# Row maxima by direct transfer, and the first head's steps first, in a pooled attention and MLP kernel

## Chip, core and metric

The kernel runs on one core of a Trainium2 chip. The metric is the time of one execution on the device in microseconds (us), as the median of several runs. The engines named below are TensorE (PE in the profile, its weight loads PEld), VectorE (DVE), ScalarE (ACT), GpSimd (POOL) and SyncE (SP), which issues every transfer.

## The reference

```python
# q, k, v: (4, 8, 1152, 64) float32; w_in: (512, 2048), w_out: (2048, 512), float64 as drawn
q_pool = q.reshape(B, H, S // 2, 2, D).mean(axis=3)          # 576 queries per head
scores = q_pool @ k.transpose(0, 1, 3, 2) / sqrt(D)          # 576 x 1152
scores = scores - max(scores, axis=-1)
attn = exp(scores); attn = attn / (sum(attn, axis=-1) + 1e-9)
x = (attn @ v) -> (4 * 576, 8 * 64) = (2304, 512)
h = x @ w_in
out = maximum(0.01 * h, h) @ w_out                           # (2304, 512)
```

## The kernel before

There are 32 heads (4 batches of 8). Matmuls run on float32r operands, and float32 accuracy is kept by splitting an operand into a high and a low part. For each head:

- `load_k`, `load_q` and `load_v` (L397, L435, L489) bring keys, queries and values. `k_tr` (L401) transposes the keys on TensorE in nine blocks of 128 keys. `k_hi` (L417) writes the rounded high part of the keys to the tile `ka`, `k_lo` (L421) the low part into the other 64 partitions: even blocks of keys have the high part in partitions 0 to 63, odd blocks in 64 to 127. `k_dup` (L425) copies the high parts to a tile `kb` by three transfers.
- `q_sum` (L454) adds pairs of queries on GpSimd, `q_tr` (L459) transposes them, `q_hi` (L470) rounds the high part into both halves of `qh`, `q_lo` (L474) writes the low part to `ql`.
- The row maxima. `qk` (L495) computes scores with queries on the partitions: four tiles of 128 consecutive queries against three thirds of the keys, and the last 64 queries, twice side by side, against two quarters from each half of the keys. `vmax` (L511) takes the maximum of each score tile on VectorE, `m_side` (L514) moves the last tile's second half of maxima on ScalarE, and `vneg` (L518) takes the negated maximum of all partial ones into `neg`, with the query on the partition and the tile number along the row. `m_tr` (L521) transposes `neg` on TensorE, `m_cp` (L525) copies five rows of 128 from the bank to `ms` on ScalarE, and `m_dma` (L529) writes them, by one transfer, to row 64 of `ql`. Row 64 of `kb` is 1, so the maximum is subtracted inside the score matmul.
- The scores again, now with keys on the partitions: `qkt` (L537, matmuls L542 and L543), `exp` (L545) on ScalarE, `esum` (L549) on GpSimd for the row sums, `pv` (L554) with the values, `r_mm` (L565) for the sums of what `esum` left, and a chain of small transfers (`r_fold`, `r_row`, `r_wide`) by which the output is divided by the sums.

The weights come as float64, are converted on ScalarE and VectorE (`w_f32`, L624) and split (`w_hi`, `w_lo`), beside the first heads. Four of nine MLP blocks (`l1`, `post`, `l2`) run beside the later heads, the others after them.

The order of the work is written out before anything runs, by a planner (`Scheduler`, L130). Each step has a priority, in units in which a head has 5, a duration that the planner assumes, steps it depends on, and buffers it takes. The planner repeatedly picks the startable step of the lowest priority and gives it to an engine that may do it. `SHIFT` (L45) adds an offset to the priority of each kind of step, by phase. Every engine then executes its instructions in that fixed order and waits on semaphores. The tag `t` stands for the two or three banks that `k_tr`, `q_tr`, `qk`, `m_tr` and `r_mm` share, `s` for the score banks of `qkt`.

Of the kernel before, what the change touches and what calls it, by code (L numbers as in the profile page):

```python
# [9 lines left out]
F32 = mybir.dt.float32  # L10
# [10 lines left out]
AHEAD = 14  # L21
MAXES = 4
# [4 lines left out]
MT = 5  # L27
# [18 lines left out]
    "esum": (-3.5, 20.75, 83.5, -27.75, -12.25),  # L46
    "exp": (27.75, 25.75, -8.25, -9, 17.25),
    "g_act": (0, 0, 6, 10),
    "g_hi": (0, 0, -18, -14),
    "g_lo": (0, 0, 13.25, -16),  # L50
    "g_mix": (0, 0, 24),
    "k_dup": (4.25, -32.25, -78.5, -3.75, 43.5),
    "k_hi": (24.5, 72.75, -4, -104, -22.5),
    "k_lo": (-45.5, -9, 0, 25.25, -34.25),
    "k_tr": (23.5, 16, 19.5, -24, 35),
    "l1": (-4.75, -27.5, -7.5),
    "l2": (-19, 22.25, 14),
# [24 lines left out]
    "r_cp": (-27.75, -22, -55, -0.5, -3),
    "r_fold": (1.75, 11, -65, -44, 19.5),
    "r_inv": (-6.25, 18.25, -2.75, 3.5, 16.5),
    "r_mm": (23, 28.5, -8.25, 2, 10.5),
    "r_row": (41.25, 19.75, -23.25, 6, 0.25),
    "r_wide": (-31.25, 0, 49.25, 7, -7.25),
    "scale": (21.25, -36.75, 8.5, 17.5, -7.5),
    "vmax": (-22.75, -29, -31, -139.5, 109.75),
    "vneg": (43.25, -29.75, 2, -29.5, -19.25),  # L90
    "w_f320": (-10, 37, -0.25, -37.5),
    "w_f321": (-37.5, 119.5, 44.75, -11.75),
    "w_f322": (-2, -36.5, 6.5, 53.5),
# [3 lines left out]
    "w_out_dma": (0.5, -1.5),
    "w_rest": (48.5, 7.5, -1.25),
    "w_sum": (-31, -3.75, 3.25),
    "w_top": (-3, -35.25, -3),  # L100
    "ws_load": (-30, -15, 45.75),
    "x_hi": (2, -12, 43.25),
    "x_lo": (-35.25, -26, 5.25),
    "x_load": (3.25, -11.75, 0.25),
    "x_out": (15.5, -21, -23.25, -41, 8),
    "zeros": (0, 58.25, -46),
}
PHASES = {"attention": (1, 2, 8, 14), "weights": (8, 16, 24), "mlp": (1, 3)}
# [21 lines left out]
class Scheduler:  # L130
# [76 lines left out]
    def start(self, s, e, at, pending):  # L207
# [44 lines left out]
def tile_pooled_attention_moe(  # L252
# [40 lines left out]
    def copy(e, out, in_):  # L293
# [4 lines left out]
    NBU = len(BURSTS)  # L298
    QTILES = [(c, min(128, SP - c)) for c in range(0, SP, 128)]
# [11 lines left out]
        "ms": (1, [NQ, 128], F32R, sb),  # L311
# [45 lines left out]
    negs = [sb.tile([128, D], F32, name=f"neg{i}") for i in range(2)]  # L357
# [51 lines left out]
    def by_half(t, x):  # L409
        return t[:, :(KT - 1) * 128].rearrange("p (a x n) -> p a x n", x=2, n=128)[:, :, x]  # L410

    def k_part(hd, x):
        if x == 2:
            return kps[hd, 1][0:64, :128], ka[hd][:, (KT - 1) * 128:], 0
        return kps[hd, 0][64 * x:64 * x + 64].rearrange("p (a n) -> p a n", n=128), by_half(ka[hd], x), 64 * x

    def k_hi(hd, x, e):  # L417
        src, d, o = k_part(hd, x)
        copy(e, d[o:o + 64], src)

# [133 lines left out]
    def pv(hd, b, e, *got):  # L554
# [304 lines left out]
    def sp(n, nbytes, run=512):  # L859
        return dict(eng={"SP": 0.45 * n}, lat=nbytes / 300e3 * max(1.0, 512 / run))  # L860

    for hd in range(NHD):
        p0 = 5.0 * hd
        pr = p0 - AHEAD
# [8 lines left out]
        for g in range(2):  # L873
# [4 lines left out]
            for x in (2,) if g else (0, 1):  # L878
                n = 128 if g else 512
                step(k_hi, hd, x, prio=pr + 0.1 * g, eng={"ACT": act(n, True)}, deps=[("k_tr", hd, g)])  # L880
                step(k_lo, hd, x, prio=pr + 0.1 * g, eng={"DVE": dve(n, psum=True)}, deps=[("k_hi", hd, x), None if g else ("k_hi", hd, 1)])
        step(k_dup, hd, prio=pr + 1, **sp(3, 0.3e6), deps=[("k_hi", hd, x) for x in range(3)], takes=[("kb", [last])])
        step(load_v, hd, prio=pr + 2, **sp(1, 0.3e6), order=after("load_v"), takes=[("vv", [("pv", hd, NBU - 1)])])
        step(load_q, hd, prio=pr - 4 - early, **sp(1, 0.3e6), order=after("load_q"), takes=[("qn", [("q_sum", hd)])])
# [6 lines left out]
        for x in range(2):  # L891
            for y in range(2):
                step(q_hi, hd, x, y, prio=pr + 0.5, eng={"ACT": act(HW, True)}, deps=[("q_tr", hd)])
# [3 lines left out]
        pm = p0 - MAXES  # L897
        ready = [("k_lo", hd, x) for x in range(3)] + [("q_hi", hd, x, y) for x in range(2) for y in range(2)]
        todo = [(i, c) for i in range(NQ) for c in range(NCH if QTILES[i][1] == 128 else 2)]
        for n, (i, c) in enumerate(todo):  # L900
            before = [("qk", hd, *todo[n - 1])] if n else after("qk", *todo[-1])
            w = CW if QTILES[i][1] == 128 else S // 4
            step(qk, hd, i, c, prio=pm + 0.02 * n, eng=mm(w) if w == CW else mm(w, w), deps=ready + before + ([] if w == CW else [("q_side", hd)]),
                 takes=[("t", [("vmax", hd, i, c)])] + ([] if n else [("st", [("m_tr", hd)])]))
            step(vmax, hd, i, c, prio=pm - 1 + 0.02 * n, eng={"DVE": dve(w, psum=True)}, deps=[("qk", hd, i, c)])
        step(m_side, hd, prio=pm - 2, eng={"ACT": act(2)}, deps=[("vmax", hd, *x) for x in todo[-2:]])
        step(vneg, hd, prio=pm - 2, eng={"DVE": 0.17}, deps=[("m_side", hd)] + [("vmax", hd, *x) for x in todo[:-2]])
# [3 lines left out]
        ready += [("k_dup", hd), ("m_dma", hd)] + [("q_lo", hd, x) for x in range(2)]  # L911
        done = ("pv", hd, NBU - 1)
        ns = KT - 1 - direct(hd)
        for t in range(KT):
# [3 lines left out]
            step(exp, hd, t, prio=p0 - 5 + 0.5 * t, eng={"ACT": act(2 * HW, True)}, deps=[("qkt", hd, t)],  # L918
# [152 lines left out]
```

## Time and profile before

| | |
|---|---|
| runs | 909.6, 913.74 and 913.08 us, median 913.08 us |
| profiled execution | 910.57 us |
| its span, from the first to the last instruction | 908.8 us |
| mean granted TensorE clock | 0.993 |
| TensorE busy | 873.0 us (96%), 6408 matmuls and as many weight loads |
| VectorE, ScalarE, GpSimd busy | 528.6 (58%), 464.0 (51%), 454.0 us (50%) |
| DMA packets | 113268, 158.73 MB; 21632 of them under 512 B |

Matmuls are pipelined, so a matmul's own length is longer than the distance between the starts of two in a row. An engine's idle time is put down to what ended it (the releaser).

### The profile page before, as it was taken

What the parts mean: (1) busy time and instruction counts of PE and PEld (TensorE: products, weight loads), DVE (VectorE), ACT (ScalarE), POOL (GpSimd) and SP (SyncE); (2) the same over time, 40 slices, a digit from 0 to 9 for tenths busy, and PEclk for the clock granted to TensorE, in tenths of its full rate; (3) what the DMA queues carried; (4) which work ended last, traced back from release to release, by engine and by line L of the source; (5) the groups of instructions that cost most, each with busy time, mean ns of one, the idle gap of its engine ahead of it and who ended that gap; (6) DMA issues with size and microseconds to landing.
All of it is one profiled execution on the core that took longest, in us unless ns stands there. A gap on an engine that the chain in (4) does not pass through costs nothing.

```text
span 908.8 us, 17344 instructions
## 1 busy us (share of the span) xinstructions
PE 873.0 (96%) x6408; PEld 731.1 (80%) x6408; DVE 528.6 (58%) x1135; ACT 464.0 (51%) x911; POOL 454.0 (50%) x351
## 2 busy tenths in 40 slices
PE   5899989899999999999999999999999999999997
PEld 3676666577778777887887787788888999999997
DVE  6788868687665455554544555404249963645443
ACT  3677777766666655555556555444124442323231
POOL 1467676686778685676667567567511010110000
PEclk9899999999999999999999999999999999999999
DMA  6478876757846764454355354444665676767670
GB/s 169 127 222 267 242 216 172 190 158 218 246 142 176 212 174 108 137 161 118 108 160 164 99 139 132 113 124 121 212 216 178 190 230 217 231 222 215 202 229 28
DMA packets 113268, 158.73 MB, mean 175 GB/s; under 512 B 21632, under 2 KB 80160, under 8 KB 113184
## 3 DMA queue, kind: packets, MB, share of 16 engines
q1 hardware_dynamic: 113184, 157.64, 58.8%
q8 instruction: 50, 0.82, 0.4%
q14 instruction: 34, 0.28, 0.1%
HBM read 130.02 MB, written 17.90 MB: 163 GB/s over the span
## 4 chain that ended last, share of the span: by engine, by line
PE 77%; DMA 9%; ACT 3%; POOL 3%; SPq 3%; issue 3%; DVE 2%; ACTq 0%; POOLq 0%; DVEq 0%
PE banks L703 21%; PE banks L560 11%; PE banks L784 11%; PE banks L509 8%; PE banks L542 7%; PE banks L543 6%; PE banks L816 3%; PE banks L818 3%; PE banks L817 3%; DMA raw<-in_moe_w_in_dram 3%; DMA ws<-wd 2%; POOL sm L552 2%; SPq L585 2%; PE banks L571 2%; PE banks L407 1%
## 5 line engine op out<-in xcount | busy, mean ns | idle before, releaser
L547 ACT ACTIVATE e<-banks 128x576 f32<-128x576 f32 x288 | 185.3, 650 | 174.3 <-PE banks L543 169.8
L552 POOL TENSOR_TENSOR sm<-sm,e 128x576 f32<-128x576 f32 x168 | 242.8, 1445 | 40.2 <-ACT e L547 31.1
L512 DVE TENSOR_REDUCE stat<-banks 128x1 f32<-128x384 f32 (+1 forms) x448 | 217.5, 534 | 71.2 <-PE banks L509 67.5
L542 PE MATMUL banks<-qh,ka 128*128 128x288 f32 x576 | 170.9, 312 | 3.0 <-ACT e L547 2.8
L543 PE MATMUL banks<-ql,kb 128*128 128x288 f32 x576 | 162.0, 297 | 1.1 <-DMA ql<-ms 1.1
L703 PE MATMUL banks<-xb,ws 128*128 128x256 f32 x1152 | 160.9, 283 | 0.8 <-DMA ws<-wd 0.7
L560 PE MATMUL banks<-e,vv 128*64 128x288 f32 x1152 | 154.1, 412 | 0.0
L703 PEld LDWEIGHTS banks<-xb,ws 128*128 128x128 f32 x1152 | 151.1, 189 | 2.6 <-DMA ws<-wd 0.9
L542 PEld LDWEIGHTS banks<-qh,ka 128*128 128x128 f32 x576 | 109.2, 190 | 28.4 <-issue 12.4
L560 PEld LDWEIGHTS banks<-e,vv 128*64 128x64 f32 x1152 | 76.8, 137 | 61.5 <-issue 15.1
L509 PE MATMUL banks<-ka,qh 128*128 128x384 f32 x384 | 115.1, 366 | 8.6 <-DVE stat L512 4.3
L423 DVE TENSOR_TENSOR ka<-banks,ka 64x512 fp32r<-64x512 f32 (+1 forms) x96 | 53.1, 554 | 104.4 <-ACT ka L294 89.0
L543 PEld LDWEIGHTS banks<-ql,kb 128*128 128x128 f32 x576 | 109.5, 190 | 2.6 <-DMA ql<-ms 1.3
L552 POOL TENSOR_TENSOR sm<-e 128x576 f32<-128x576 f32 x32 | 46.2, 1444 | 86.1 <-ACT e L547 86.0
L509 PEld LDWEIGHTS banks<-ka,qh 128*128 128x128 f32 x384 | 68.1, 194 | 23.8 <-DVE stat L512 10.4
L703 PE MATMUL banks<-ka,ws 128*128 128x256 f32 x576 | 71.9, 280 | 1.4 <-DMA ws<-wd 1.4
L703 PEld LDWEIGHTS banks<-ka,ws 128*128 128x128 f32 x576 | 69.8, 188 | 2.0 <-DMA ws<-wd 1.8
L784 PE MATMUL banks<-wo,gg 128*128 128x256 f32 x312 | 59.9, 282 | 0.0
L472 ACT ACTIVATE qh<-banks 64x288 fp32r<-64x288 f32 x128 | 51.7, 404 | 3.5 <-PE banks L465 2.1
L294 ACT CAST ka<-banks 64x512 fp32r<-64x512 f32 (+1 forms) x96 | 45.0, 470 | 13.7 <-PE banks L407 12.6
L457 POOL TENSOR_TENSOR qs<-qn 96x384 f32<-96x384 f32 x32 | 32.0, 1000 | 34.2 <-PE banks L465 22.0
L784 PEld LDWEIGHTS banks<-wo,gg 128*128 128x128 f32 x312 | 46.9, 188 | 0.1
(177 smaller groups left out, 1220.2 us busy)
## 6 DMA issues: line engine op xcount, KB each, us to landing
ws<-wd SPq DMA_DIRECT2D x144, 512.0 KB
kn<-in_k_dram SPq DMA_DIRECT2D x32, 288.0 KB
qn<-in_q_dram SPq DMA_DIRECT2D x32, 288.0 KB
vv<-in_v_dram SPq DMA_DIRECT2D x32, 288.0 KB
kb<-ka SPq DMA_DIRECT2D x64, 128.0 KB
raw<-in_moe_w_in_dram SPq DMA_DIRECT2D x16, 512.0 KB
wd<-ws SPq DMA_DIRECT2D x16, 512.0 KB
raw<-in_moe_w_out_dram SPq DMA_DIRECT2D x16, 512.0 KB
```

The lines of the kernel that those rows point to most:

```text
L294: ENG[e].copy(out=out, in_=in_) if e == "ACT" else ENG[e].tensor_copy(out=out, in_=in_)
L423: nc.vector.tensor_tensor(out=d[64 - o:128 - o], in0=src, in1=f32(d[o:o + 64]), op=ALU.subtract)
L472: nc.scalar.activation(out=q_half(qh[hd], x)[64 * y:64 * y + 64], in_=src, func=AF.Copy, scale=QSCALE)
L509: nc.tensor.matmul(p, lhsT=lhsT, rhs=ka[hd][:, k0:k0 + w], start=(j == 0), stop=(j == 128 // n - 1))
L512: nc.vector.tensor_reduce(out=mx[hd][:, i, c:c + 1], in_=mps.pop((hd, i, c)), axis=AX.X, op=ALU.max)
L542: nc.tensor.matmul(p[:, hf, :HW], lhsT=ka[hd][:, ks], rhs=qh[hd][:, c], start=True, stop=False)
L543: nc.tensor.matmul(p[:, hf, :HW], lhsT=kb[hd][:, ks], rhs=ql[hd][:, c], start=False, stop=True)
L547: nc.scalar.activation(out=ex[hd, t], in_=sps.pop((hd, t))[:, :, :HW], func=AF.Exp)
L552: ENG[e].tensor_tensor(out=sm[hd], in0=ex[hd, 0] if t == 1 else sm[hd], in1=ex[hd, t], op=ALU.add)
L560: nc.tensor.matmul(p[64 * hf:64 * hf + 64, :HW], lhsT=vv[hd][:, t, :], rhs=ex[hd, t][:, hf], start=(t == 0), stop=(t == KT - 1),)
L703: nc.tensor.matmul(p, lhsT=wst[i, f][:, a, c, :], rhs=xx[i][x][:, c, :], start=(n == 0), stop=(n == 3 * KC - 1))
L784: nc.tensor.matmul(o, lhsT=g[i, p][:, a], rhs=w[:, x], start=(p == 0 and n == 0 and half == 0), stop=(p == FH - 1 and n == 2), skip_group_ ...
```

## The change

The transpose and the copy of the maxima (`m_tr`, `m_cp`, the tile `ms`) go. `neg` is 8 columns wide instead of 64, and `m_dma` writes from it straight to the row by two transfers. To let 4 adjacent values of one partition lie side by side in the row, tile i of `qk` consists of the queries i, i + 4, i + 8 and so on, so its stationary operand has a step of four columns. Keys are laid out as two contiguous halves (even blocks, then odd blocks, the ninth block shared between them), so `k_dup` takes two transfers, the remainder is done in two pieces by `k_hi` and `k_lo`, and `pv` takes the value blocks in that order (`TILES`). `qk` goes through the first third of the keys for all tiles, then the side tile, then the last and the middle third, each with only the parts of the keys that it needs; `m_side` no longer waits for other maxima. For head 0, the priorities of preparation and maxima are lowered by 200, `load_q` comes first of all, and `k_hi` and `q_hi` may run on VectorE as well. Exponentials are kept in order. The planner assumes 0.5 us for an issue (0.45 before), another price for changing the array's tiling, and all of `SHIFT` has new values.

```diff
+START = 200
-MT = 5
+MBYTES = 0.2e6
...
+TILINGS = {"pv": 1, "r_mm": 2, "qkr": 3}
...
-            tiled = s.key[0] in ("pv", "r_mm")
-            if tiled and not self.tiled:
-                end = self.free[e] = end + SWITCH
-            self.tiled = tiled
+            tiling = TILINGS.get(s.key[0], 0)
+            if tiling != self.tiled:
+                end = self.free[e] = end + SWITCH / 2
+            self.tiled = tiling
...
+    TILES = [*range(0, KT, 2), *range(1, KT, 2)]
...
-    negs = [sb.tile([128, D], F32, name=f"neg{i}") for i in range(2)]
+    negs = [sb.tile([128, 8], F32, name=f"neg{i}") for i in range(2)]
...
+        if x < 2:
+            return kps[hd, 0][64 * x:64 * x + 64], ka[hd][:, 640 * x:640 * x + 512], 64 * x
+        y = x - 2
+        return kps[hd, 1][0:64, 64 * y:64 * y + 64], ka[hd][:, 512 + 64 * y:576 + 64 * y], 64 * y
...
-        nc.sync.dma_start(out=d[0:64, (KT - 1) * 128:], in_=s[0:64, (KT - 1) * 128:])
         for x in range(2):
-            nc.sync.dma_start(out=by_half(d, x)[0:64], in_=by_half(s, x)[64 * x:64 * x + 64])
+            c = slice(x * S // 2, (x + 1) * S // 2)
+            nc.sync.dma_start(out=d[0:64, c], in_=s[64 * x:64 * x + 64, c])
...
-                lhsT = qh[hd][:, o:o + n]
+                lhsT = qh[hd][:, i:n * (NQ - 1):NQ - 1]
...
-        nc.sync.dma_start(out=f32(ql[hd])[64:65].rearrange("p (i n) -> p i n", n=128), in_=f32(mst.pop(hd)))
+        row, full = f32(ql[hd])[64:65], 128 * (NQ - 1)
+        nc.sync.dma_start(out=row[:, :full].rearrange("o (n i) -> o n i", i=NQ - 1), in_=mng[hd][:, :NQ - 1])
+        nc.sync.dma_start(out=row[:, full:SP].rearrange("o (n i) -> o n i", i=1), in_=mng[hd][:SP - full, NQ - 1:NQ])
...
-        pr = p0 - AHEAD
+        pr = p0 - AHEAD - (0 if hd else START)
...
-        todo = [(i, c) for i in range(NQ) for c in range(NCH if QTILES[i][1] == 128 else 2)]
+        todo = [(i, 0) for i in range(NQ)] + [(NQ - 1, 1)] + [(i, c) for c in (2, 1) for i in range(NQ - 1)]
...
-        step(m_tr, hd, prio=pm - MT, eng=trs(128), deps=[("vneg", hd)], takes=[("t", [("m_cp", hd)])])
-        step(m_cp, hd, prio=pm - 2, eng={"ACT": act(128, True)}, deps=[("m_tr", hd)], takes=[("ms", [("m_dma", hd)])])
-        step(m_dma, hd, prio=pm - 2, **sp(1, 0.01e6), deps=[("m_cp", hd)], order=[("q_lo", hd, x) for x in range(2)])
+        step(m_dma, hd, prio=pm - 2, **sp(2, MBYTES), deps=[("vneg", hd)], order=[("q_lo", hd, x) for x in range(2)])
```

## Rows read from the trace of the kernel before

**Rows 1.** The page's first part: busy us, share of the span, instructions.

```profile
PE 873.0 (96%) x6408; PEld 731.1 (80%) x6408; DVE 528.6 (58%) x1135; ACT 464.0 (51%) x911; POOL 454.0 (50%) x351
```

**Rows 2.** Windows: length, busy us (instructions) per engine, granted clock, DMA share, GB/s.

```profile
0.00:28.00 28.00, 16.99 (x54) 11.31 (x55) 19.62 (x41) 12.69 (x30) 7.36 (x17) 0.90 0.62 158
20.00:24.00 4.00, 1.10 (x6) 0.65 (x7) 3.41 (x7) 3.27 (x10) 1.24 (x2) 0.78 0.52 145
24.00:29.00 5.00, 4.96 (x16) 3.62 (x15) 4.17 (x9) 3.17 (x9) 2.00 (x3) 0.50 0.25 71
28.00:220.00 192.00, 177.83 (x1299) 130.16 (x1298) 148.74 (x302) 136.15 (x278) 128.45 (x100) 0.99 0.72 206
```

**Rows 3.** Timeline of the start: start, length, engine, line, operation, idle before.

```profile
3.76 1.30 PE L407 MATMUL banks<-ident,kn 128*128 128x128 f32 x5 [3.76 <-DMA kn<-in_k_dram]
...
5.68 1.00 POOL L457 TENSOR_TENSOR qs<-qn 96x384 f32<-96x384 f32 x1 [4.37 <-DMA qn<-in_q_dram]
...
8.54 1.65 ACT L472 ACTIVATE qh<-banks 64x288 fp32r<-64x288 f32 x4
...
10.24 0.69 PE L509 MATMUL banks<-ka,qh 128*128 128x384 f32 x1 [1.69 <-ACT qh L472]
...
12.36 6.21 DVE L512 TENSOR_REDUCE stat<-banks 128x1 f32<-128x384 f32 x13
...
23.52 0.17 DVE L519 TENSOR_REDUCE neg<-stat 128x5 f32<-128x20 f32 x1
...
24.56 0.86 SPq L530 DMA_DIRECT2D ql<-ms  x1
...
27.33 0.44 PE L543 MATMUL banks<-ql,kb 128*128 128x288 f32 x1
```

**Rows 4.** Timeline of TensorE around the transpose of a later head.

```profile
453.33 0.40 PE L818 MATMUL banks<-wo,gg 128*128 128x512 f32 x1
...
453.56 0.27 PE L523 MATMUL banks<-ident,neg 128*64 128x128 f32 x1
...
453.90 0.40 PE L817 MATMUL banks<-wo,gg 128*128 128x512 f32 x1
```

**Rows 5.** TensorE's waits, whole span: us in total, times, longest.

```profile
PE banks L571 <- DVE ka L423: 3.4, 2, 1.9
PE banks L523 <- DVE neg L519: 3.2, 2, 2.0
...
PE banks L543 <- DMA ql<-ms: 1.1, 1, 1.1
...
PE banks L509 <- ACT ms L527: 0.4, 1, 0.4
```

**Rows 6.** TensorE's waits from 30 to 120 us.

```profile
PE banks L523 <- DVE neg L519: 2.0, 1, 2.0
```

**Rows 7.** SP's issues by line: ns shortest/median/longest, first and last start.

```profile
L429 SPq DMA_DIRECT2D kb<-ka x32: 476/524/1417, 7.1 to 596.8; - x32
...
L431 SPq DMA_DIRECT2D kb<-ka x64: 596/630/1712, 7.7 to 598.1; - x64
...
L530 SPq DMA_DIRECT2D ql<-ms x32: 753/773/861, 24.6 to 594.8; - x32
...
L585 SPq DMA_DIRECT2D rt<-rs x128: 501/586/1906, 43.8 to 644.1; - x128
```

**Rows 8.** The chain that ended last: start, us, what.

```profile
41.76 3.86 DMA ql<-ms
...
133.68 2.78 DMA rt<-rs
...
736.25 2.88 PE banks L703 x24
```

**Rows 9.** Groups by line and shape: count, busy us, mean ns.

```profile
L423 DVE TENSOR_TENSOR ka<-banks,ka 64x128 fp32r<-64x128 f32 x32 | 9.1, 284 | 7.7 <-ACT ka L294 7.0
```

**Rows 10.** The chain from 30 to 60 us.

```profile
46.86 0.52 PE banks L509 x3
```

More of the change, by code (lines that the diff above doesn't have):

```diff
@@ L97 @@
[L97 to L106, printed above, removed]
+    "esum": (0.5, 61, 71.75, -32.75, -53),
+    "exp": (44.25, 43, -35.5, -33.25, 53.25),
+    "g_act": (0, 0, 7.25, 10),
+    "g_hi": (0, 0, -14, -26),
+    "g_lo": (0, 0, 12.5, -7),
@@ new lines @@
+    "g_mix": (0, 0, 24),
+    "k_dup": (52.5, -32.25, -76.5, -2.5, 43.5),
+    "k_hi": (1.25, 72.75, -3.25, -124.25, -20.5),
+    "k_lo": (-0.25, -8.25, -3.5, 10.25, -71),
+    "k_tr": (-12, 24, 21.25, -45.25, 35),
+    "l1": (-8.75, -33.75, -7),
+    "l2": (9.5, 14.75, -11),
+    "l2s": (0, 0, -4.5, 16.5),
+    "load_k": (-1, -9, 24.75, 0, 25.5),
+    "load_q": (7.5, -26.25, 47.25, -39.75, -8),
+    "load_v": (32.75, 20.5, 20.25, -4.25, -14),
+    "m_dma": (26.25, -50, -39.75, 31.75, 37.25),
+    "m_side": (-22.5, -35, 3, 10.25, 4.75),
@@ new lines @@
+    "norm": (-7.25, 91.5, 24.25, -34.5, 29.75),
+    "o_evac": (-4, 131.5, 9.25),
+    "o_mix": (0, 0, 6, 16),
+    "o_mix_out": (0, 0, 45, 32),
+    "o_out": (7, 1.5, 14.75),
+    "post0": (7, -13, -4.75),
+    "post1": (-0.75, -19.25, -10.75),
+    "post2": (-32.75, 0, 19.5),
+    "pv": (6.5, 128.5, 14, 119, -4),
+    "q_hi": (47, 5.5, 22.5, -78.5, -21),
+    "q_lo": (1, 37, -4.5, 6.5, 23),
+    "q_side": (37, -4, 51.5, -192.75, -1.75),
+    "q_sum": (-10.5, -8.5, 39.75, -74, -54.25),
+    "q_tr": (17.5, 30.25, -32, -13.5, -5.5),
@@ new lines @@
+    "qk": (-22.75, -4, 106.5, 51, 6.5),
+    "qkt": (120.75, 1.75, 146.5, 32, -37),
+    "r_cp": (-31.5, -19.5, -56, -36.25, -6.5),
+    "r_fold": (5.75, 7, -60.25, -31.5, 10.5),
+    "r_inv": (13.5, 17.75, 5.25, 35.25, 16.5),
+    "r_mm": (65.75, 6.5, -5, 1.75, 11.5),
+    "r_row": (53.25, 4.5, -23.25, 14.5, 16.25),
+    "r_wide": (-29.75, 16, 16.75, 23, -7.25),
+    "scale": (21.25, -52.75, 24.75, 40.25, 20.75),
+    "vmax": (-0.5, -10.25, -23, -93.5, 39.25),
+    "vneg": (0, -57, 2, -27, -19.25),
@@ new lines @@
+    "w_f320": (-9, 15, 15, -80),
+    "w_f321": (-41.5, 105.5, 60.25, -11.75),
+    "w_f322": (-1.5, -52.5, 28.75, 5.25),
+    "w_hi": (-73, -27, 47.75, 27.75),
+    "w_lo": (116.25, -19.5, -17, -44.25),
+    "w_load": (-10.25, 59, 73.75, -1.75),
+    "w_out_dma": (59.5, -28),
+    "w_rest": (48.5, 84, 5.25),
+    "w_sum": (-19.75, -66, -4.75),
+    "w_top": (-1, -39.25, -11),
+    "ws_load": (-40, -17.5, 45.75),
+    "x_hi": (84.75, -11.5, 43.25),
+    "x_lo": (-39.75, -10.25, 2.75),
+    "x_load": (7.5, -11.75, 4.25),
@@ L878, in tile_pooled_attention_moe @@
             for x in (2,) if g else (0, 1):
[L879 to L882, printed above, removed]
+                at, dt = (2 * act(64, True), 2 * dve(64, psum=True)) if g else (act(512, True), dve(512, psum=True))
+                step(k_hi, hd, x, prio=pr + 0.1 * g, eng={"ACT": at, "DVE": dt} if hd == 0 else {"ACT": at}, deps=[("k_tr", hd, g)])
+                step(k_lo, hd, x, prio=pr + 0.1 * g, eng={"DVE": dt}, deps=[("k_hi", hd, x)])
+        step(k_dup, hd, prio=pr + 1, **sp(2, 0.3e6), deps=[("k_hi", hd, x) for x in range(3)], takes=[("kb", [last])])
         step(load_v, hd, prio=pr + 2, **sp(1, 0.3e6), order=after("load_v"), takes=[("vv", [("pv", hd, NBU - 1)])])
-        step(load_q, hd, prio=pr - 4 - early, **sp(1, 0.3e6), order=after("load_q"), takes=[("qn", [("q_sum", hd)])])
+        step(load_q, hd, prio=pr - 4 - early if hd else -1e3, **sp(1, 0.3e6), order=after("load_q"), takes=[("qn", [("q_sum", hd)])])
         step(q_sum, hd, prio=pr - 1, eng=pool(QT * D, "q_sum"), lock=True, deps=[("load_q", hd)], order=after("q_sum"), takes=[("qs", [("q_tr", hd)])])
@@ L917, in tile_pooled_attention_moe @@
             b = [n for n, x in enumerate(BURSTS) if x[0] <= t < x[1]][0]
-            step(exp, hd, t, prio=p0 - 5 + 0.5 * t, eng={"ACT": act(2 * HW, True)}, deps=[("qkt", hd, t)],
+            step(exp, hd, t, prio=p0 - 5 + 0.5 * t, eng={"ACT": act(2 * HW, True)}, deps=[("qkt", hd, t)], order=[("exp", hd, t - 1)] if t else after("exp", KT - 1),
                  takes=[("e", [("pv", hd, b), ("esum", hd, max(t, 1)) if t <= ns else ("r_mm", hd)])])
```

105 lines of the change are left out of this document (26 added, 79 removed).

## Prediction

> **What bounds the kernel now.** I read the page's busy shares first, then the windows by stage, then who TensorE waited for, then the first 30 us in order of time, and last single prices. TensorE is busy 873.0 of 908.8 us [rows 1]; no other compute engine passes 58%. So the span is TensorE's work plus its idle time, and a change is worth something only if it takes instructions from TensorE or closes one of its gaps. The idle time is 35.8 us in all. The windows give where: 28.00 - 16.99 = 11.0 us before 28 us, 192.00 - 177.83 = 14.2 us from 28 to 220 us (attention beside the conversion of the weights, with VectorE at 148.74 and ScalarE at 136.15 of 192 us), and the other 10.6 us after that [rows 2]. From 220 us on TensorE has hardly a gap. [...]
>
> In the first 28 us the reader is to see a chain of one head. Keys land at 3.76; the query load, issued second, lets GpSimd start its sum only at 5.68; ScalarE rounds the queries in four steps from 8.54 to 10.19; the first score matmul is at 10.24. From then VectorE sets the pace: 13 maxima in 6.21 us, 0.478 us each. They are over at 18.57, yet the negation (L519) runs only at 23.52, the transfer of the maxima is issued at 24.56, and the first matmul that uses them (L543) is at 27.33 [rows 3].
>
> **The change part by part.**
> *The transpose of the maxima (L523) goes, 32 times.* Its 0.27 us is a pipelined length, so I take its price from starts: from L818 at 453.33 past the transpose at 453.56 to L817 at 453.90 is 0.57 us for two 512-column matmuls and the transpose [rows 4]. 512 columns start 0.23 us apart there (453.33 to 453.56), so the transpose holds TensorE for 0.57 - 0.46 = 0.11 to 0.12 us. At 0.12 us, 31 of them outside the start give 3.7 us, on the path since TensorE is the bound. Bounds: 0 (it filled gaps), and 31 x 0.27 = 8.4 us.
>
> *The waits around it go.* TensorE executes in order, so while L523 waited for the negation everything behind it stood: 3.2 us in two waits, of which 2.0 us lie between 30 and 120 us [rows 5, 6]. It waited 0.4 us for ScalarE's copy of the maxima to free a bank, and 1.1 us, once, for the maxima to land [rows 5]. That is 3.5 us outside the start. What is late next is partly the same VectorE queue, which feeds the score matmuls too; I take half, 1.7 us, bounds 0 and 3.5.
>
> *The start.* The queries are now loaded first. By the rows, the first load (the keys now) is used at 3.76 and the second at 5.68 [rows 3]. So the sum of the queries (1.0 us) runs from about 3.7, transposes (0.7) to 5.5, four rounding steps of 0.41 us on two engines to 6.3; keys from 5.7, transposes 1.1 to 6.8, high part 0.6 to 7.4, low part 0.7 to 8.1 (each step at the length it had in the same stretch). The first score matmul moves from 10.24 to about 8.1. Then 16 maxima at 0.478 are 7.6 us, with about 2.8 us of this head's other VectorE steps among or before them: negation at 18.5 to 18.7 instead of 23.52, because the low parts of heads 1 and 2 and the copy of the side maxima no longer stand ahead of it. Two issues of 0.59 us (the length of an issue of 24-byte pieces [rows 7]) end at 19.9 and land some 2 us later, near 21.8: 5.5 us before 27.33. But TensorE had used part of that time for later heads (transposes of keys for heads 2 and 3, four score matmuls of head 1), about 3 us at full pace. Some of it still fits between maxima; I charge 1.0 us and take 4.5 us. [...]
>
> *The maxima as a transfer of small pieces.* Before: one issue of 0.77 us [rows 7] for five pieces of 512 bytes. After: 128 pieces of 16 bytes and 64 of 4 bytes, in two issues. The nearest row is the sums' fold (L585), 192 pieces of 24 bytes in four issues per head at 0.59 us; on the chain it takes 2.78 us from issue to landing, while the old transfer of maxima took 3.86 us from issue to landing in a busy stretch [rows 7, 8]. So the load on the queues, not the piece, sets the landing. One of 32 heads waited for the maxima at all [rows 5], so I count 0. Bounds: 0, and about 1 us for each of the first few heads, 3 us. On the way there ScalarE's copy goes too.
>
> *Keys in contiguous halves.* The copy (L429, L431) goes from three issues (0.52 + 2 x 0.63 = 1.78 us of SP) to two (about 1.2), and from 576 pieces of 512 bytes to 128 of 2,304. SP: -0.6 us here, about +0.4 for the second issue of maxima, so about even, and everything queued behind them on SP moves by under 0.5 us. The small remainder is now two steps instead of one on ScalarE and on VectorE: VectorE's step of 128 columns costs 0.284 us [rows 9], two of 64 at most 0.57, so up to 9 us over 32 heads, spread beside TensorE's work; without that cover (the 12 heads before 220 us) up to 12 x 0.28 = 3.4 us. I count 0.
>
> *Every fourth query as stationary operand.* The 384 score matmuls now load columns 16 bytes apart. No row shows such a load. From one side: with contiguous columns, 24 matmuls of 256 columns and as many loads take 2.88 us, 0.12 us a pair [rows 8], so a load costs at most 0.12 us and is hidden at that. Score matmuls of 384 columns start 0.173 us apart (0.52 us for three) [rows 10]. A load up to 1.4 times as long stays hidden: 0 us. From the other side: twice 0.12 is 0.24, 0.067 us more than the pace, 384 times: 26 us. I take 0, because the row that bounds the load at 0.12 is no more than an upper bound. [...]
>
> *Order of score tiles, ordered exponentials, new shifts.* A score tile on the first third of the keys waits for one low part instead of three, and the side maxima are formed early, so ScalarE's copy leaves the end of the chain. The rest is a rearrangement of the same work; bounds: -8 us (about half of the 14.2 us of idle time closed) and +23 us (below); I count 0.
>
> **Sum.** 3.7 + 1.7 + 4.5 = 9.9 us. The profiled execution took 910.57 us for its span of 908.8, so 900.7; it is 2.5 us below the median of the runs, 913.08, from which the sum gives 903.2. I say 902.
>
> **Rivals.** Times from 912, between the two.
> (a) *The start is given back.* Head 0 is earlier, but its gain is lost by head 1, whose maxima need VectorE for about 10 us more. For: VectorE sets the pace from 11 to 18 us [rows 3]. Against: before, head 1's maxima waited another 3.9 us in flight [rows 8], and VectorE has gaps, 19.62 us busy of 28 [rows 2]. Only the transposes stay: 912 - 3.7 = 908.
> (b) *The strided loads show.* Slower: place, each of the 384 score matmuls; price up to 26 us; it cancels the 9.9 us when a pair takes 0.026 us more than now, 0.20 instead of 0.173. At its full price: 912 - 9.9 + 26 = 928. For: it is the one new form on the engine that is the bound. Against: loads of 128 columns fit beside 256-column matmuls, and these have 384.
> (c) *The new order brings in-order waits.* TensorE stood 3.4 us in two waits at L571 for a VectorE step [rows 5], up to 1.9 us each. One such wait for each of the 12 heads before 220 us is 23 us: 912 - 9.9 + 23 = 925; from five on the gain is gone.
> (d) *The idle stretch from 28 to 220 us closes by half as well,* as banks and ScalarE steps are freed: 902 - 8 = 894.
>
> **How the numbers follow.** Forecast 0.55 (own range 897 to 908), (a) 0.17, (b) 0.07, (c) 0.13, (d) 0.08. A measurement of this kernel tells about 0.5% from no change, 4.6 us: faster is below 908.5. Faster: 0.50 of the forecast, all of (d), 0.05 of (a): 0.63. Slower: (b) and 0.09 of (c): 0.16. The rest, 0.21, is the same. The range 888 to 916 leaves out most of (b), the worse half of (c), and the low end of (d), some 0.16.
>
> **What would show it.** L523 and L527 absent; the first L543 near 22 instead of 27.33 and the first score matmul near 8; TensorE idle before 28 us down from 11.0 by some 4; score matmuls still 0.173 us apart in a run (0.20 and over is rival b); no wait of L543 for the maxima past head 1; idle time from 28 to 220 us at or below 14. If that stretch is above 20, (c) holds, and if the first L543 is not before 25, the start failed.

## The result, and the profile after

The kernel is slower: 921.77 us, median of four runs (920.96 to 924.67), beside 913.41 us before (909.6 to 914.3) on the same chip. The ratio is 1.0113, with a 95% interval of 1.0087 to 1.0139. The forecast of 902 us and its range up to 916 both missed.

The page's first part and the windows of the kernel after answer to [rows 1] and [rows 2]. Columns of the windows: length, busy us (instructions) of TensorE, its loads, VectorE, ScalarE and GpSimd, granted clock, DMA share, GB/s.

```profile
PE 895.8 (97%) x6376; PEld 764.5 (83%) x6376; DVE 531.1 (58%) x1165; ACT 464.4 (50%) x912; POOL 452.1 (49%) x352
```

```profile
0.00:28.00 28.00, 16.51 (x55) 12.37 (x55) 19.23 (x43) 12.47 (x31) 6.91 (x16) 1.00 0.57 158
...
24.00:34.00 10.00, 8.49 (x33) 7.00 (x31) 6.83 (x15) 6.62 (x15) 5.70 (x6) 1.00 0.50 147
...
28.00:220.00 192.00, 185.65 (x1271) 144.62 (x1270) 148.23 (x310) 132.77 (x273) 126.71 (x99) 0.99 0.68 198
220.00:700.00 480.00, 478.49 (x3265) 394.10 (x3266) 239.67 (x528) 251.64 (x510) 308.27 (x235) 1.00 0.53 152
```

TensorE has 32 instructions fewer, yet 22.8 us more of busy time. Its idle time fell at the same time: the span is 920.0 us, so 24.2 us are idle, where 35.8 were. From 28 to 220 us 6.35 us are idle instead of 14.2; before 28 us it is 11.5 us, where it was 11.0, so the start gave TensorE nothing. So the added work is larger than the added time, and part of it lies where TensorE used to stand. The groups by line and shape say which work it is: the score matmuls of `qk`, first in the kernel after (count, busy us, mean ns, then idle time before and what ended it), then in the kernel before.

```profile
L514 PE MATMUL banks<-ka,qh 128*128 128x384 f32 x384 | 137.9, 439 | 7.0 <-ACT qzs L490 2.7 <-DVE stat L517 2.2 <-DVE ka L424 1.2
L514 PEld LDWEIGHTS banks<-ka,qh 128*128 128x128 f32 x384 | 106.0, 319 | 19.4 <-issue 6.0 <-DVE stat L517 5.9 <-ACT qzs L490 3.0
```

```profile
L509 PE MATMUL banks<-ka,qh 128*128 128x384 f32 x384 | 115.1, 366 | 8.6 <-DVE stat L512 4.3 <-ACT qh L472 1.7 <-ACT rs L577 0.9
L509 PEld LDWEIGHTS banks<-ka,qh 128*128 128x128 f32 x384 | 68.1, 194 | 23.8 <-DVE stat L512 10.4 <-ACT qh L472 2.6 <-DVE ka L423 2.3
```

The load of 128 columns takes 319 ns instead of 194. The chain from 300 to 340 us gives the price of a pair:

```profile
299.83 0.74 PE banks L514 x3
...
301.04 0.13 PE banks L542
```

Three score matmuls in a run take 0.74 us, 0.247 each; in [rows 10] it was 0.52, 0.173 each. That is 0.074 us more, 384 times: 28 us of TensorE. The neighbouring 288-column matmul keeps its 0.13 us.

The start answers to [rows 3] (timeline: start, length, engine, line, operation, idle before), the kernel after first, then lines of the kernel before that [rows 3] does not have:

```profile
3.87 0.99 POOL L458 TENSOR_TENSOR qs<-qn 96x384 f32<-96x384 f32 x1 [2.56 <-DMA qn<-in_q_dram]
...
9.12 1.10 PE L514 MATMUL banks<-ka,qh 128*128 128x384 f32 x2 [2.72 <-ACT qzs L490]
...
17.21 0.17 DVE L524 TENSOR_REDUCE neg<-stat 128x5 f32<-128x20 f32 x1
...
18.61 0.59 SPq L530 DMA_DIRECT2D ql<-neg  x1
...
23.37 0.44 PE L543 MATMUL banks<-ql,kb 128*128 128x288 f32 x1
...
25.88 1.66 ACT L475 ACTIVATE qh<-banks 64x288 fp32r<-64x288 f32 x4
...
26.98 1.10 PE L514 MATMUL banks<-ka,qh 128*128 128x384 f32 x2 [1.21 <-DVE ka L424]
...
27.56 1.19 ACT L547 ACTIVATE e<-banks 128x576 f32<-128x576 f32 x2
...
32.71 0.44 PE L542 MATMUL banks<-qh,ka 128*128 128x288 f32 x1
...
32.95 0.44 PE L543 MATMUL banks<-ql,kb 128*128 128x288 f32 x1
...
33.96 2.16 PE L560 MATMUL banks<-e,vv 128*64 128x288 f32 x16
```

```profile
24.59 2.71 PE L509 MATMUL banks<-ka,qh 128*128 128x384 f32 x4
...
27.09 0.44 PE L542 MATMUL banks<-qh,ka 128*128 128x288 f32 x1
...
28.29 0.65 ACT L547 ACTIVATE e<-banks 128x576 f32<-128x576 f32 x1 [1.66 <-PE banks L543]
...
32.08 2.16 PE L560 MATMUL banks<-e,vv 128*64 128x288 f32 x16
```

The negation is 6.3 us earlier (17.21, before 23.52) and the first L543 4.0 us (23.37, before 27.33). The first exponential, which was at 28.29, is only 0.7 us earlier: ScalarE rounds parts of later heads until 27.54. Head 1's first score matmul is 2.4 us later (26.98, before 24.59), behind a VectorE step on the keys, and the first matmul with the values, L560, is 1.9 us later (33.96, before 32.08).

### The profile page after: what moved, and what is told of

Same layout as the page of the kernel before. It is cut to its first block, busy times and chain, and to the rows that moved or that the text cites. A ratio compares the mean times of both kernels' runs of the same rounds, so it can differ in the third digit from the quotient of the medians.

```text
span 920.0 us, 17359 instructions
## 1 busy us (share of the span) xinstructions
PE 895.8 (97%) x6376; PEld 764.5 (83%) x6376; DVE 531.1 (58%) x1165; ACT 464.4 (50%) x912; POOL 452.1 (49%) x352
## 4 chain that ended last, share of the span: by engine, by line
PE 86%; DMA 5%; DVE 3%; ACT 3%; issue 2%; POOL 1%; SPq 1%; DVEq 0%; ACTq 0%; POOLq 0%
PE banks L703 22%; PE banks L560 13%; PE banks L514 11%; PE banks L784 11%; PE banks L542 8%; PE banks L543 7%; PE banks L816 3%; PE banks L817 3%; PE banks L818 3%; PE banks L571 2%; PE banks L407 2%; DMA qn<-in_q_dram 1%; DMA xb<-xd 1%; DMA raw<-in_moe_w_out_dram 1%; DMA raw<-in_moe_w_in_dram 1%
## 5 line engine op out<-in xcount | busy, mean ns | idle before, releaser
L517 DVE TENSOR_REDUCE stat<-banks 128x1 f32<-128x384 f32 (+1 forms) x448 | 220.3, 536 | 98.7 <-PE banks L514 95.6
L542 PE MATMUL banks<-qh,ka 128*128 128x288 f32 x576 | 171.6, 313 | 2.6 <-ACT e L547 2.5
L543 PE MATMUL banks<-ql,kb 128*128 128x288 f32 x576 | 162.9, 298 | 0.0
L560 PE MATMUL banks<-e,vv 128*64 128x288 f32 x1152 | 153.8, 412 | 0.0
L514 PE MATMUL banks<-ka,qh 128*128 128x384 f32 x384 | 137.9, 439 | 7.0 <-ACT qzs L490 2.7
L542 PEld LDWEIGHTS banks<-qh,ka 128*128 128x128 f32 x576 | 111.3, 193 | 28.4 <-issue 12.8
L560 PEld LDWEIGHTS banks<-e,vv 128*64 128x64 f32 x1152 | 77.0, 136 | 55.5 <-issue 10.0
L514 PEld LDWEIGHTS banks<-ka,qh 128*128 128x128 f32 x384 | 106.0, 319 | 19.4 <-issue 6.0
L543 PEld LDWEIGHTS banks<-ql,kb 128*128 128x128 f32 x576 | 110.4, 192 | 2.0
L424 DVE TENSOR_TENSOR ka<-banks,ka 64x64 fp32r<-64x64 f32 (+1 forms) x128 | 58.0, 453 | 27.5 <-ACT ka L294 25.1
L481 DVE SCALAR_TENSOR_TENSOR ql<-banks,qh 64x288 fp32r<-64x288 f32 x64 | 29.0, 453 | 61.7 <-ACT qh L475 61.0
L294 ACT CAST ka<-banks 64x512 fp32r<-64x512 f32 (+1 forms) x127 | 49.4, 390 | 11.3 <-PE banks L407 6.0
```

The lines of the kernel that those rows point to most:

```text
L294: ENG[e].copy(out=out, in_=in_) if e == "ACT" else ENG[e].tensor_copy(out=out, in_=in_)
L514: nc.tensor.matmul(p, lhsT=lhsT, rhs=ka[hd][:, k0:k0 + w], start=(j == 0), stop=(j == 128 // n - 1))
L517: nc.vector.tensor_reduce(out=mx[hd][:, i, c:c + 1], in_=mps.pop((hd, i, c)), axis=AX.X, op=ALU.max)
L542: nc.tensor.matmul(p[:, hf, :HW], lhsT=ka[hd][:, ks], rhs=qh[hd][:, c], start=True, stop=False)
L543: nc.tensor.matmul(p[:, hf, :HW], lhsT=kb[hd][:, ks], rhs=ql[hd][:, c], start=False, stop=True)
L560: nc.tensor.matmul(p[64 * hf:64 * hf + 64, :HW], lhsT=vv[hd][:, TILES[t], :], rhs=ex[hd, t][:, hf], start=(t == 0), stop=(t == KT - 1),)
```

## The experiments

Each is compared with the kernel before on the same chip. In 1 to 3, 7 to 10 and 12 to 15 the score tiles and the row do not agree on the order of queries, so a query is given another one's maximum (in 15 the tiles also overlap); nothing else of the work is left out. "..." stands for parts of an edit that are not shown.

**1. Contiguous loads in the kernel after.**

```diff
-                lhsT = qh[hd][:, i:n * (NQ - 1):NQ - 1]
+                lhsT = qh[hd][:, o:o + n]
```

> The changed kernel with one edit: each score tile's stationary operand is 128 consecutive queries instead of every fourth, so the loads are contiguous; the row that is subtracted then belongs to another query of the same head, all else, the order of the work too, is as in the changed kernel. Theory S (the strided loads cost): in the changed kernel's chain three score matmuls take 0.74 us, 0.247 each, against 0.173 before; 0.074 x 384 = 28 us too much. Expect 0.173 to 0.18 again, weight loads of this line back from 319 to about 190 ns, and a time of 894 to 902 us, faster than the kernel before by 11 us or more. Rival O (the new order and its waits cost, the loads hide): the time stays at 915 or above.

907.68 us; ratio 0.993 (0.9914 to 0.9946). Page, groups, one window and chain of this kernel:

```profile
PE 868.5 (96%) x6376; PEld 729.7 (81%) x6376; DVE 528.7 (58%) x1165; ACT 463.3 (51%) x912; POOL 452.3 (50%) x352
```

```profile
L514 PE MATMUL banks<-ka,qh 128*128 128x384 f32 x384 | 108.3, 357 | 11.5 <-DVE stat L517 6.5 <-ACT qzs L490 2.7 <-DVE ka L424 1.5
L514 PEld LDWEIGHTS banks<-ka,qh 128*128 128x128 f32 x384 | 66.6, 190 | 27.5 <-DVE stat L517 12.9 <-issue 6.1 <-ACT qzs L490 3.0
```

```profile
28.00:220.00 192.00, 178.84 (x1297) 131.16 (x1298) 147.61 (x312) 135.16 (x280) 130.47 (x101) 0.99 0.71 202
```

```profile
327.74 0.52 PE banks L514 x3
```

One slice takes 27.3 us off TensorE's busy time (895.8 to 868.5) and 14.1 us off the time (15.1 us if each is taken beside the kernel before on its own chip). The load is back at 190 ns, the pace, from the start of one matmul to the start of the next, at 0.173 us. The idle time is back too: the span is 904.6, so 36.1 us, 11.9 more than in the kernel after. Nearly half of the price of the strided loads had been paid with idle time. That is also why the time did not come down to the 894 to 902 us expected.

**2. Strided loads in the kernel before.**

```diff
-                lhsT = qh[hd][:, o:o + n]
+                lhsT = qh[hd][:, i:n * (NQ - 1):NQ - 1]
```

> The kernel before with the opposite edit alone: stationary operand every fourth query, so the maxima in the row belong to other queries; order and transfers as before. Theory S: 0.247 us per score matmul in a run, up to 28 us more, of which some lies in gaps (14 us of idle time between 28 and 220 us): 931 to 941 us. Rival O: no change, 910 to 916 us.

929.38 us; ratio 1.0171 (1.0149 to 1.0192), about 15 us more, a little less than expected.

```profile
L509 PEld LDWEIGHTS banks<-ka,qh 128*128 128x128 f32 x384 | 108.1, 317 | 17.6 <-DVE stat L512 8.2 <-ACT qh L472 2.4 <-ACT e L547 1.8
```

Its load takes 317 ns and TensorE is busy for 899.5 of 926.5 us, 26.5 more than in [rows 1]. The same edit with the opposite sign, in the other order of work, has nearly the same price.

**3 and 15. A step of two and of three queries in the kernel after.**

```diff
-                lhsT = qh[hd][:, i:n * (NQ - 1):NQ - 1]
+                lhsT = qh[hd][:, 256 * (i // 2) + i % 2:256 * (i // 2) + 256:2]   # experiment 3
+                lhsT = qh[hd][:, 48 * i:48 * i + 382:3]                           # experiment 15
```

> The changed kernel with a step of two queries (8 bytes) in the stationary operand instead of four (16 bytes); the row's maxima belong to other queries. [...] If any step above one costs the same: 0.247 us, 920 to 924 us. Rival O: 915 or above whatever the step.

> The changed kernel with a step of three queries (12 bytes) in the stationary operand, overlapping tiles; the row's maxima belong to other queries. Step four costs 0.247 us per score matmul, step two 0.173 to 0.18. [...]

Step two: 907.24 us, ratio 0.9916 (0.989 to 0.9941), as without a step. Step three: 911.75 us, a single run. The load's group in each and a run of three in the chain:

```profile
L514 PEld LDWEIGHTS banks<-ka,qh 128*128 128x128 f32 x384 | 69.5, 200 | 25.5 <-DVE stat L517 11.2 <-issue 5.5 <-ACT qzs L490 3.0
```

```profile
334.36 0.53 PE banks L514 x3
```

```profile
L514 PEld LDWEIGHTS banks<-ka,qh 128*128 128x128 f32 x384 | 85.8, 258 | 23.7 <-DVE stat L517 9.7 <-issue 5.5 <-ACT qzs L490 3.0
```

```profile
309.66 0.57 PE banks L514 x3
```

| step of the stationary operand | load, ns | three score matmuls in a run, us |
|---|---|---|
| 1 (4 bytes) | 190 | 0.52 |
| 2 (8 bytes) | 200 | 0.53 |
| 3 (12 bytes) | 258 | 0.57 |
| 4 (16 bytes) | 319 | 0.74 |

The price isn't that of any stride: two are nearly free, and what comes after grows by some 60 ns a step. The loads still overlap the matmuls (at step three a load takes 258 ns and a pair 0.19 us), so the pace moves clearly only from step three on, to 0.19 us and at step four to 0.247.

**4. The maxima in pieces of 4 bytes, contiguous loads.** Five transfers of one column of `neg` each, and the planner told so.

```diff
...
-        nc.sync.dma_start(out=row[:, :full].rearrange("o (n i) -> o n i", i=NQ - 1), in_=mng[hd][:, :NQ - 1])
+        for i in range(NQ - 1):
+            nc.sync.dma_start(out=row[:, 128 * i:128 * i + 128].rearrange("o (n i) -> o n i", i=1), in_=mng[hd][:, i:i + 1])
...
```

> The changed kernel with contiguous loads (consecutive queries in a tile) and the maxima brought to their own places in the row by five transfers of 4-byte pieces, 576 pieces per head instead of 192, and the planner told five issues. Theory S: as e1, 894 to 904 us, if three more issues on SP and the pieces stay hidden; the first score matmuls of a head should not wait for the maxima. Rival P (small pieces cost): slower than e1 by 5 us or more, with waits for the maxima.

941.01 us; ratio 1.029 (1.0232 to 1.0348). The landing of the pieces does not explain it: it takes 3.1 us (median), that of the 16-byte pieces in the kernel after 2.8, and no wait of TensorE for maxima shows in the trace. A wait of TensorE (us, times, longest; this kernel has one line more, so L543 is L542 elsewhere) and a window:

```profile
PE banks L543 <- ACT e L548: 13.9, 13, 2.9
```

```profile
28.00:220.00 192.00, 171.91 (x1158) 126.27 (x1158) 131.88 (x287) 123.67 (x256) 115.58 (x90) 0.93 0.64 176
```

TensorE waits for exponentials in a newly planned order, and its mean granted clock in this stretch is 0.93. The edit changes the order and puts three more issues a head on SyncE, so it does not measure the piece, and its two parts are not told apart.

**5. A step of two with a row that fits it.** Two transfers of 8-byte pieces and one of 4-byte ones, the planned order kept, so each query has its own maximum and the loads are cheap.

```diff
+                lhsT = qh[hd][:, 256 * (i // 2) + i % 2:256 * (i // 2) + 256:2]
...
+        for j in range(2):
+            nc.sync.dma_start(out=row[:, 256 * j:256 * j + 256].rearrange("o (n i) -> o n i", i=2), in_=mng[hd][:, 2 * j:2 * j + 2])
```

> The changed kernel with every second query of 256 in a score tile (a step of 8 bytes) and the maxima brought to their own places by two transfers of 8-byte pieces and one of 4-byte pieces, three issues instead of two; the planner's assumptions, and so the order, stay those of the changed kernel. Theory S (only the 16-byte step cost, and pieces are free): as e3, 904 to 910 us, faster than the kernel before. Rival P (small pieces or the third issue cost, as e4's 941 us could mean): 915 us or more, with TensorE waiting for the maxima.

914.97 us (12 runs); ratio 1.0024 (1.0001 to 1.0046). It repairs 7 of the 8 us that the change lost, and does not beat the kernel before. Beside experiment 3 it has one issue more per head in the same order and is 7.7 us slower: TensorE waits 8.2 us in 11 waits of L543 for exponentials (5.5 in ten there, at L542), and 1.3 us, once, for the maxima. Experiment 10 also has one issue more per head in an unchanged order, and loses too. Whether SyncE's time for the issue costs this, or any disturbance of the order, no experiment tells apart.

**6. Transpose, copy and `ms` put back into experiment 1.**

```diff
...
+        step(m_tr, hd, prio=pm - MT, eng=trs(128), deps=[("vneg", hd)], takes=[("t", [("m_cp", hd)])])
+        step(m_cp, hd, prio=pm - 2, eng={"ACT": act(128, True)}, deps=[("m_tr", hd)], takes=[("ms", [("m_dma", hd)])])
+        step(m_dma, hd, prio=pm - 2, **sp(1, 0.01e6), deps=[("m_cp", hd)], order=[("q_lo", hd, x) for x in range(2)])
...
```

> e1 (contiguous loads, new order, new key halves) with the transpose on TensorE, the copy on ScalarE and the single transfer put back, with their old shifts; the planner makes a new order from it. If the direct transfer is worth what the prediction said (3.7 us of transposes and 1.7 of waits): 911 to 915 us, TensorE busy 4 us longer than in e1's 868.5. If it is worth nothing: 906 to 909 us.

916.11 us (12 runs); ratio 1.0022 (1.0 to 1.0045): 8 us above experiment 1. That is over twice the transposes' price, so the newly planned order may have its part.

**7. No precedence for the first head, in experiment 1.**

```diff
-START = 200
+START = 0
...
-        step(load_q, hd, prio=pr - 4 - early if hd else -1e3, **sp(1, 0.3e6), order=after("load_q"), takes=[("qn", [("q_sum", hd)])])
+        step(load_q, hd, prio=pr - 4 - early, **sp(1, 0.3e6), order=after("load_q"), takes=[("qn", [("q_sum", hd)])])
...
```

> e1 without the first head's precedence: no lowering by 200, queries not loaded first, rounding on ScalarE alone for head 0. In e1 the first exponential started at 27.27 us against 28.29 in the kernel before, since ScalarE had the rounding of heads 1 and 2 ahead of it; so theory W (the precedence is worth about 1 us): 907 to 910 us. Rival, as predicted (4.5 us or more): 911 to 914 us.

919.1 us; ratio 1.0077 (1.0047 to 1.0108). But its first exponential is at 25.04 and its first `pv` at 30.72 us, both earlier than in experiment 1 (27.27 and 32.48). The kernel with the earlier start is the slower one; neither of the two expected outcomes came.

**8. The direct transfer alone, planned anew in the kernel before.** `m_tr` and `m_cp` go, nothing else.

```diff
...
-        step(m_dma, hd, prio=pm - 2, **sp(1, 0.01e6), deps=[("m_cp", hd)], order=[("q_lo", hd, x) for x in range(2)])
+        step(m_dma, hd, prio=pm - 2, **sp(2, 0.01e6), deps=[("vneg", hd)], order=[("q_lo", hd, x) for x in range(2)])
```

> The kernel before with the direct transfer alone: no transpose, no copy, two transfers of small pieces; tiles of consecutive queries, so the maxima in the row belong to other queries. If the transposes and waits are what the change gives back: 913 - 5 = 907 to 910 us. If small pieces or the second issue cost as much as the transposes did: 912 to 916 us.

923.32 us; ratio 1.0111 (1.0075 to 1.0147). That is slower than either outcome expected. TensorE waits 13.4 us in 13 waits for exponentials, and 3.0 us in three for the maxima.

**9. Experiment 1 again, on another chip.**

> e1 once more (the changed kernel with contiguous loads), as the measure for the others of this call: 905 to 910 us, ratio to the kernel before 0.990 to 0.996. If it comes out at 912 or above, e1's gain was the chip's and not the kernel's.

907.97 us (7 runs); ratio 0.9927 (0.9901 to 0.9954). The gain without the stride is real. Its profiled execution, though, has TensorE busy for 874.6 of 910.2 us, beside 868.5 of 904.6 in experiment 1.

**10. The direct transfer in the kernel before's own order.** `m_tr` and `m_cp` stay in the plan and issue nothing.

```diff
     def m_tr(hd, e, i):
-        mtp[hd] = p = new("t", i)
-        nc.tensor.transpose(p[0:D, 0:128], mng[hd], ident)
+        pass
...
```

> The kernel before with the direct transfer, in the order that the planner makes for the kernel before: it still plans the transpose and the copy, but they issue nothing, and the two transfers stand where the one stood; the row's maxima belong to other queries. e8 had the same instructions in a newly planned order and took 923 us. Theory D (the direct transfer gains what the prediction took for transposes and waits, 3.7 + 1.7 us, and e8 lost by its new order): 906 to 910 us. Rival (the transfer itself costs): 915 us or more.

920.12 us (12 runs); ratio 1.0056 (1.0036 to 1.0077). Windows, and TensorE's waits:

```profile
44.00:48.00 4.00, 1.97 (x8) 1.56 (x8) 3.07 (x7) 0.79 (x2) 0.00 (x0) 0.83 0.89 189
48.00:50.00 2.00, 2.00 (x9) 2.00 (x9) 0.69 (x2) 1.60 (x3) 0.22 (x1) 0.50 0.69 217
...
144.00:148.00 4.00, 1.05 (x3) 0.87 (x4) 1.88 (x6) 1.01 (x3) 3.52 (x3) 0.71 0.46 136
148.00:152.00 4.00, 4.00 (x18) 3.90 (x17) 2.75 (x6) 2.52 (x5) 0.51 (x1) 0.50 0.56 158
```

```profile
PE banks L509 <- DVE stat L512: 9.0, 10, 3.4
...
PE banks L543 <- DMA ql<-neg: 3.4, 2, 2.0
```

With 32 instructions fewer and the order unchanged the kernel loses. The waits for maxima and score tiles open gaps (1.05 of 4 us busy from 144 us on), and behind some of them TensorE runs at a granted clock of 0.50 for some us. Four such places show between 32 and 220 us; in the kernel before it was one, from 138 to 142 us.

**11. A step of three in the moving operand, kernel before.** The keys of a third are interleaved; the maxima over all thirds stay the same.

```diff
-            nc.tensor.matmul(p, lhsT=lhsT, rhs=ka[hd][:, k0:k0 + w], start=(j == 0), stop=(j == 128 // n - 1))
+            nc.tensor.matmul(p, lhsT=lhsT, rhs=ka[hd][:, c:c + 3 * (w - 1) + 1:3] if n == 128 else ka[hd][:, k0:k0 + w], start=(j == 0), stop=(j == 128 // n - 1))
```

> The kernel before with the keys of a score matmul taken as every third (a step of 12 bytes in the moving operand; the maxima are the same), the stationary operand contiguous. [...]

948.55 us; ratio 1.0372 (1.0344 to 1.04). The groups and the chain of this kernel:

```profile
L509 PE MATMUL banks<-ka,qh 128*128 128x384 f32 x384 | 171.3, 522 | 3.0 <-ACT qh L472 1.5 <-DVE stat L512 0.9 <-DVE ka L423 0.2
L509 PEld LDWEIGHTS banks<-ka,qh 128*128 128x128 f32 x384 | 68.9, 195 | 20.7 <-DVE stat L512 5.6 <-ACT qh L472 1.9 <-DVE ka L423 1.8
```

```profile
315.13 0.68 PE banks L509 x2
```

Now the matmul is longer and the load is not: two in a run take 0.68 us in its chain, 0.34 each. In the moving operand a step of three doubles the time from start to start; in the stationary one it adds 10%.

**12. The first head's scores and exponentials put first as well, in experiment 1.**

```diff
-            step(qkt, hd, t, prio=p0 + 0.5 * t, ...
+            step(qkt, hd, t, prio=p0 + 0.5 * t - (0 if hd else START), ...
```

(and `exp` likewise)

> e1 with the scores and the exponentials of head 0 lowered by 200 as well. In e1 head 0's first scores are done at 23.6 us, but its first exponential starts at 27.27, behind fourteen rounding steps of heads 1 and 2 on ScalarE. Theory W (this is where the start's gain went): first exponential near 24 us and 1 to 4 us less than e9, if the newly planned order loses nothing elsewhere. Rival: the later heads pay for it, same as e9 or slower.

923.82 us; ratio 1.0091 (1.006 to 1.0122). The first exponential is at 24.50 and the first `pv` at 28.87 us, the earliest of all, and the time is 16 us above experiment 9.

**13. The table `SHIFT` of the kernel before in experiment 1.**

> e1 (the changed kernel with contiguous loads) with the SHIFT table of the kernel before; the table has no entry that is missing for a step that is left. Theory F (what e1 gains, 6.5 us, lies in shifts fitted to the new steps, since the transfer alone in the old order gained nothing in e10): 914 us or more. Rival (the new steps gain by themselves, in any order): 904 to 910 us.

920.12 us; ratio 1.0084 (1.0054 to 1.0114). With the same steps, the offsets alone are worth 12 us against experiment 9 (on another chip).

**14. Idle matmuls on TensorE while the first head waits, in experiment 1.**

```diff
...
+    def warm(n):
+        if ("qkt", 0, 0) not in sch.done:
+            for _ in range(n):
+                nc.tensor.transpose(banks[:, 1, :128], ident, ident)
...
```

> e1 with idle matmuls on TensorE (128 columns against the identity, into a bank nobody uses yet) before and between head 0's steps, until its first scores. In e1 the first scores of head 0 run at 0.24 us a matmul, half pace, to about 31 us, after TensorE had been idle more than half of the start. Theory C (the clock costs the start 1 to 3 us): pace 0.13 in those scores, 1 to 3 us less than e9's 908. Rival (ScalarE sets the start, its first exponential at 27.27 us): 907 to 909 us, no difference.

907.08 us (8 runs); ratio 0.9931 (0.9906 to 0.9957), as experiment 9. Its busy time before 28 us is 22.75 instead of 16.32 us, and nothing comes of it in the median. Its first scores (here L550 and L551) and exponentials (L555):

```profile
26.29 0.30 PE L551 MATMUL banks<-ql,kb 128*128 128x288 f32 x1
...
26.43 0.29 PE L550 MATMUL banks<-qh,ka 128*128 128x288 f32 x1
...
29.35 1.19 ACT L555 ACTIVATE e<-banks 128x576 f32<-128x576 f32 x2
```

From 26.29 us on the matmuls are 0.13 to 0.14 us apart, so the half pace is gone. But they come some 3 us later than in the kernel after (26.29 beside 23.37), among the added matmuls, and the first exponential 1.8 us later (29.35 beside 27.56). So this doesn't show what the half pace costs: its gain and that delay are not told apart. The expectation's "idle more than half of the start" is a little high: in experiment 1 TensorE is busy for 12.99 of the first 24 us.

## Why the prediction was wrong

**The step that failed** is "Every fourth query as stationary operand", taken at 0 of 0 to 26 us. It is 14 to 15 us of time (experiments 1 and 2) and 26 to 28 us of TensorE. The rest of the change gained 6 to 7 us, which leaves the 8 us that it lost. Rival (b) happened, and its test, a pace of 0.20 and over, reads 0.247. The bound of 26 us assumed a load of twice 0.12 us, and the pair did come to 0.247. What was wrong was the choice inside the bounds: I took the low end because the row for contiguous loads was only an upper bound, but a row with contiguous columns says nothing of a strided load. Rival (b) had a chance of 0.07. Even so, its full price showed by little more than half: of the 36.1 us for which TensorE stands idle without the stride, the longer score matmuls took up 11.9. Being the bound 96% of the time is not the same as every us showing.

**The transposes, 3.7 us.** They are gone. TensorE's busy time is 4.5 us lower in experiment 1 than before, but 1.6 higher in experiment 9, which is the same kernel: the term has about the size by which busy time differs between two executions, and isn't told apart from it.

**The waits around them, 1.7 us.** Not gained. Without the stride the idle time is 36.1 us (experiment 1) and 35.6 (experiment 9), before 35.8. The two waits at L523 are gone, but the score matmuls wait longer for VectorE's maxima; here the kernel before, then experiment 1:

```profile
PE banks L509 <- DVE stat L512: 4.3, 6, 1.4
```

```profile
PE banks L514 <- DVE stat L517: 6.5, 7, 2.1
```

This is the "what is late next" that I had charged with half.

**The start, 4.5 us.** It was given back, as in rival (a): before 28 us TensorE is idle for 11.5 us instead of some 7. The first score matmul was due at 8.1 and came at 9.12. The negation was due at 18.5 to 18.7 and came at 17.21, because I counted 16 maxima where a head has 14 (twelve for the four tiles, two for the last queries): 0.96 us less gives 17.5 to 17.7. The first L543 was due at 21.8 and came at 23.37, behind other work on TensorE. Rival (a) named VectorE and head 1, and head 1 is later by 2.4 us, behind VectorE. What the step left out is ScalarE: its rounding for later heads now stands ahead of the first exponentials, and the first L560 comes later than before. And TensorE's 288-column matmuls start 0.24 us apart until 33 us (32.71 to 32.95), while they take 0.13 later: the half pace of 24 to 29 us, where the granted clock was 0.50 [rows 2], did not go, it lasted longer. Experiments 7 and 12 go further: first exponentials and values earlier by 2 to 4 us than in experiment 1 belong to kernels that are slower by 11 to 16. They were planned anew, so this doesn't show that an early start costs, but it shows that its us don't arrive at the end by themselves.

**The small pieces, 0.** Right for the kernel after: they land in 2.8 and 2.4 us (median of 32 each), no later than the 2.78 to 3.86 of [rows 8], and no wait of L543 for them shows. In other orders it is not always 0: experiments 8 and 10 wait 3.0 and 3.4 us for the maxima, about the 3 us of the upper bound. **Keys in halves, 0:** not tried by itself. In the kernel after the score matmuls wait 2.1 us in two waits for VectorE's steps on the keys, 0.8 us in two before, so a small price is not excluded.

**Order and shifts, 0 of -8 to +23.** Without the stride the whole change is worth 6 to 7 us (experiments 1, 9 and 14), near rival (a)'s 908. Experiment 13 shows that this hangs on the offsets that came with these steps. Rival (c) did not happen: without the stride 13.2 us are idle from 28 to 220 us (experiment 1; 15.0 in experiment 9), below the 20 of its sign. Rival (d) did not either: those 6.35 us of the kernel after were closed by the longer score matmuls (and half of 14.2 is 7.1 us, not 8). Of the experiments that planned a new order under offsets made for other steps (4, 6, 7, 8, 12, 13) none ended below the kernel before. So the share of each part of these 6 to 7 us stays open: taking one part away changes the order too, and the order can be worth more than the part.

## What to carry to other kernels

Before changing an operand's layout to help another step, price its reading on the engine that is the bound: a step of two four-byte columns in the stationary operand was nearly free, four made each pair 0.074 us slower, and here that was more than everything that the change saved. When a new form has wide bounds and no row of its own, the low end is not the default. In a kernel whose order was fitted to its steps, test a part in the unchanged order and look at the gaps; a newly planned order can bring some 10 us of its own (experiment 13: 12 us).

## What the hardware showed that I had not expected

- The step has another price for each operand: in the stationary one 190, 200, 258 and 319 ns per load at steps 1 to 4; in the moving one a step of three takes the pace from 0.173 to 0.34 us, with the load unchanged at 195 ns.
- A gap in the middle of the kernel can cost twice. After a stretch in which TensorE was busy for 1.05 of 4 us, it ran the next 4 us at a granted clock of 0.50 (experiment 10, 144 to 152 us). In the kernel before, behind 1.40 us of idle time, 288-column matmuls start 0.24 us apart (140.52 and 140.76 us, granted clock 0.57 from 138 to 142 us), and 0.13 again at 142.20 and 142.33 us. This is not so behind every gap: behind another (0.32 of 2 us busy from 186 us) the clock reads 1.00 from 188 to 192 us.
- The granted clock of a window can disagree with the pace. From 24 to 34 us the window of the kernel after says 1.00, while 288-column matmuls start 0.24 us apart, as they did in the kernel before at 27.09 and 27.33 us, where the granted clock is 0.50 [rows 2, 3]. In experiment 15 the same stretch, with as many matmuls in the same busy time (33 in 8.49 us), reads 0.50:

```profile
24.00:34.00 10.00, 8.49 (x33) 6.96 (x31) 6.83 (x15) 6.63 (x16) 5.74 (x6) 0.50 0.48 143
```
